# Delta-rule attention and SwiGLU on one core: the first group's diagonal blocks as 64x32 products of their own, one transpose, and other engines for beta's products and two clearings

## The chip, the cores and the metric

The kernel runs on one core of one Trainium2 chip. The metric is the device time of one execution in microseconds. A kernel is judged by the median of its runs; the profile is one more execution, recorded by the hardware profiler.

Engine names in the views: PE is TensorE (PEld its weight loads), DVE is VectorE, ACT is ScalarE, POOL is GpSimd, SP is SyncE, which here only issues DMAs. L444 is line 444 of the kernel file.

## The reference, cut to what matters

```python
# q, k, v: (4, 8, 768, 48), beta: (4, 8, 768), float32
def attn(q, k, v, beta):
    k_n = k / (np.linalg.norm(k, axis=-1, keepdims=True) + 1e-06)
    state = zeros((B, H, D, D))
    for t in range(S):
        kt, vt, bt = k_n[:, :, t], v[:, :, t], beta[:, :, t, None]
        y[:, :, t] = einsum('bhd,bhde->bhe', q[:, :, t], state)
        v_old = einsum('bhde,bhd->bhe', state, kt)
        state = state + bt[..., None] * einsum('bhd,bhe->bhde', kt, vt - v_old)
    return y
# bridge: (B, H, S, D) -> x of (3072, 384); then
def moe(x, w_gate, w_val, w_out):           # 384 -> 1536 -> 384
    g = x @ w_gate
    return (g / (1 + exp(-g))) * (x @ w_val) @ w_out
```

## The kernel before, in words

The sequence of 768 steps is cut into 12 chunks of C = 64 steps; two chunks make a group. Four batches with eight heads are 32 recurrences. Within a chunk the recurrence is solved with the triangular matrix of the keys' products: the Gram matrix K K' of each recurrence's chunk (64 x 64) is scaled by beta and inverted as a unit triangular matrix. The inverse is made in 32 x 32 blocks (R = 32): the two diagonal blocks of a chunk by forward substitution on VectorE, all recurrences of a group at a time, one per partition, and the block below the diagonal by two rounds of small products on TensorE (`join_late`, L561 to L592).

**The start, which the change touches.** It is written out by hand under a manual schedule (from L1094), so each engine executes its instructions in the order of the code. Group 0 goes first:

- The keys of chunks 0 and 1 are loaded, and beta in 16 small DMAs, eight on POOL's queue and eight on SP's (`load_beta`, L377). VectorE forms the keys' squared norms (`norms`, L353, L361), GpSimd takes their square root as a power of 0.5 (L365).
- TensorE turns the keys (L432), ScalarE copies them to SBUF (L434), and `gram` (L444) makes the 64 x 64 Gram matrices of both chunks: 32 matmuls a chunk with 64 x 64 stationary tiles, of which four are in use (two halves of the rows, two halves of the columns). A float32 matmul leaves two records in the trace.
- L472 copies them from PSUM into `a_sb`, for group 0 in the layout (i, chunk, head), one strided copy for each bank: three on VectorE and one on ScalarE.
- `turn` (L479) brings the diagonal blocks into the form in which one partition holds one recurrence: a transpose over 128 partitions (L482) for one half, and two over 32 partitions each (L485) for the other.
- `first_n` (L386 to L390) makes the reciprocal norms from GpSimd's result, L1128 copies beta out of the place it was loaded to, `divide_beta` (L369) multiplies beta twice by the reciprocal norm, and `scale_m` clears `zb` and puts beta on its diagonal (GpSimd, L497, L498), negates beta (L500) and scales `mb` with it (L502).
- `substitute` (L510) is 31 steps of two VectorE instructions each (L515, L521), every one waiting for the one before it. After 17 of the steps, four small instructions (L246) that prepare the weights' conversion are put between.
- `late_z` (L552, L558) transposes the result into `zt` and `d_t`; `join_late` starts on TensorE with L568, then L580; ScalarE copies the blocks (L588); then come `advance(0)` (L716, L735, L747) with the first chunk's outputs, their transposes (L780, L783), and the first gate products (L800).

While that goes on, TensorE turns q and the next keys (L432), makes their products (L444), and turns group 1's diagonal blocks by 32 x 32 products with the identity (`turned_m`, L544). The weights arrive as 64-bit floats, as pairs of words; `convert` (L246 to L296) makes float32 of them with VectorE and ScalarE.

**The rest.** From the first gate product on, TensorE works through the feed-forward products of every chunk: gate and value (L800), output (L829, L912). Between them, `fill` and `point` put steps of the recurrence of later chunks and of the next groups' inverses, in an order fixed at build time.

PSUM has eight banks: the pairs `px` and `py`, and four banks `ffn`. The Gram products of chunks 0 and 1 use `px` and `py`, and the turned keys of chunks 2 and 3 come next in the same two pairs.

The start as it stands in the code, from L1115:

```python
        copy_a, copy_v = nc.scalar.copy, nc.vector.tensor_copy
        turned(0, False)
        turned(1, False, "py")
        gram(0, False)
        gram(1, False, "py", (copy_a, copy_v))
        mb = new_mb()
        ...
        r_b = first_n()
        copy_v(beta_b, beta_s.rearrange("p (g r) -> p g r", g=NG)[:, :, 0:R])
        ...
        divide_beta(0, r_b)
        zb = scale_m(mb, [(slice(0, R), mb)], beta_b[:, 0])
        nc.gpsimd.memset(ztp[0], 0.0)
```

Of the kernel before, what the change touches and what calls it, by code (L numbers as in the profile page):

```python
# [21 lines left out]
def kernel(  # L22
# [350 lines left out]
    def load_beta(at, queue=nc.gpsimd):  # L373

        s_, blk, c, par = at // 8, at // 4 % 2, at // 2 % 2, at % 2
        lo, m = 64 * c + R * blk, (NG - 1) * 128 + R
        queue.dma_start(  # L377
            out=beta_s[8 * at : 8 * at + 8, 0:m],
            in_=beta.rearrange("(bp b) (j par) s -> b par bp j s", b=2, par=2)[
                s_ ^ par, par, :, :, lo : lo + m  # L380
            ],
        )

    def first_n():
        n = n_t[0].rearrange("p c h -> p (c h)")
        nc.vector.tensor_scalar_add(n, n, 1e-6)  # L386
        r_n = work.tile([128, R], FP32, name="r_n", tag="n_b", bufs=1)
        nc.vector.reciprocal(r_n, n)
        r_b = work.tile([128, R], FP32, name="r_b", tag="nb", bufs=1)
        nc.vector.transpose(r_b, r_n)  # L390
        return r_b
# [46 lines left out]
    def gram_steps(c, of_q, tag=None, copies=(nc.vector.tensor_copy,) * 2):  # L438

        xt = (qt if of_q else kt)[c]  # L440
        p_g = banks("p_g", tag or ("py" if of_q else "px"))
        p_v = [p.rearrange("p (bp j i) -> p bp j i", bp=NB, j=NJ) for p in p_g]
        for bp, j, par, b, _ in every():
            nc.tensor.matmul(  # L444
                p_v[par][half_of(b if of_q else b ^ par), bp, j],
                kt[c][half_of(par), bp, j, b],
                xt[half_of(par), bp, j, b],
            )
        if of_q:
            p_sb[c] = work.tile([128, 2, NB, NJ, C], FP32, name="p_sb", bufs=2)  # L450
        elif c % 2 == 0:
            a = work.tile([128, C * 2 * HH], FP32, name="a_sb")

            a_sb[c // 2] = (
                a.rearrange("p (i c h) -> p c h i", c=2, h=HH)
                if c == 0
                else a.rearrange("p (c h i) -> p c h i", c=2, h=HH)
            )
            a_of[c // 2] = a
        yield  # L460
        for par in range(2):
            p_h = p_g[par].rearrange("p (h i) -> p h i", i=C)
            if of_q:
                nc.vector.tensor_tensor(
                    out=p_sb[c][:, par].rearrange("p bp j i -> p (bp j) i"),
                    in0=p_h,
                    in1=mask_q[:, None, :].to_broadcast([128, HH // 2, C]),
                    op=ALU.mult,
                )
            else:  # L470
                at = slice(par * HH // 2, (par + 1) * HH // 2)
                copies[par](a_sb[c // 2][:, c % 2, at], p_h)  # L472
        yield

    def gram(*args):
        for _ in gram_steps(*args):
            pass

    def turn(out, in_):  # L479


        nc.vector.transpose(out(slice(0, 128), 1), in_(slice(0, 128), 1))  # L482
        yield
        for rows in (slice(0, 32), slice(64, 96)):
            nc.vector.transpose(out(rows, 0), in_(rows, 0))  # L485
            yield
# [23 lines left out]
    def substitute(mb, zb):  # L510
        for j in range(R - 1):
            m = R - 1 - j
            tmp = work.tile([128, 256], FP32, name="tmp", bufs=1)
            t_v = tmp[:, 0 : (j + 1) * m].rearrange("p (k i) -> p k i", i=m)
            nc.vector.tensor_tensor(  # L515
                out=t_v,
                in0=zb[:, 0 : j + 1, j : j + 1].to_broadcast([128, j + 1, m]),
                in1=mb[:, j : j + 1, j + 1 : R].to_broadcast([128, j + 1, m]),
                op=ALU.mult,
            )  # L520
            nc.vector.tensor_tensor(  # L521
                out=zb[:, 0 : j + 1, j + 1 : R],
                in0=zb[:, 0 : j + 1, j + 1 : R],
                in1=t_v,
                op=ALU.add,
            )
            yield

    def recur(p, m=D):
        p = p[:, :, 0 : NB * NJ * m]  # L530
# [556 lines left out]
    with tc.manual_schedule(  # L1087
# [9 lines left out]
        for at in range(0, 16, 2):  # L1097
            load_beta(at)
            load_beta(at + 1, nc.sync)
        norms(0)  # L1100

        nc.vector.memset(places[0][:, 0:1], 0)
# [12 lines left out]
        copy_a, copy_v = nc.scalar.copy, nc.vector.tensor_copy  # L1115
        turned(0, False)
        turned(1, False, "py")
        gram(0, False)
        gram(1, False, "py", (copy_a, copy_v))
        mb = new_mb()  # L1120
        a_v = a_of[0].rearrange("p (i m) -> p i m", i=C)
        for _ in turn(
            lambda rows, half: mb[rows],
            lambda rows, half: a_v[rows, R * half : R * half + R],
        ):
            pass
        r_b = first_n()
        copy_v(beta_b, beta_s.rearrange("p (g r) -> p g r", g=NG)[:, :, 0:R])  # L1128
        for n in range(12, 17):
            stage(n)  # L1130
        load_v(1)
        divide_beta(0, r_b)
        zb = scale_m(mb, [(slice(0, R), mb)], beta_b[:, 0])
        nc.gpsimd.memset(ztp[0], 0.0)

        turned(0, True, "ffn")
        turned(2, False, "px")
# [111 lines left out]
```

## Time and profile before

| what | value |
|---|---|
| median of 8 runs | 749.32 us (747.34 to 750.08) |
| profiled execution | 749.11 us |
| its span, first to last instruction | 747.4 us |
| busy in the span | PE 709.0, PEld 616.3, DVE 475.4, ACT 149.4, POOL 68.0 us |
| mean granted clock of TensorE | 0.961 |
| first substitution step (L515) starts | 22.92 us after the span's start |
| last substitution step (L521) ends | 46.92 us |
| first product of the join (L568) starts | 49.09 us |
| first gate product (L800) starts | 66.87 us |

The profile page gives busy time by engine, the span in 40 slices, the chain of work that ended last, and groups of instructions with what their engine waited for. Queries of the same trace give the chain in order of time, all instructions of a window in order of time (start, duration, engine, line, operation, then in brackets the idle time before it and what ended that), the waits summed by pair, and busy time and granted clock by window. Times there count from the span's start. The profiled execution's own time is 1.7 us above its span. The granted clock of a window is a share of TensorE's full clock.

### The profile page before, as it was taken

The page shows a single profiled execution, that of the slowest core. Times are in us where ns is not written, and L with a number is a line of the kernel's source. Part 1 is how long each engine was busy: PE and PEld are TensorE (multiplying, and loading weights), DVE is VectorE, ACT ScalarE, POOL GpSimd, SP SyncE. Part 2 cuts the span into 40 slices and gives each one's busy share as a digit, 9 for nine tenths or more (in the row PEclk, how much of TensorE's full clock was granted, in tenths as well). Part 3 has the DMA queues.
Part 4 walks back from the last instruction along what each step waited for, and adds up shares of the span by engine and source line. Part 5 has one row for each costly group of instructions (what it writes and reads, how often), then busy time and mean ns, then how long its engine had stood idle before and what let it go on. Part 6 is the DMA issues. An engine that isn't in the chain of part 4 may idle for free.

```text
span 747.4 us, 22217 instructions
## 1 busy us (share of the span) xinstructions
PE 709.0 (95%) x10004; PEld 616.3 (82%) x10004; DVE 475.4 (64%) x981; ACT 149.4 (20%) x277; POOL 68.0 (9%) x46
## 2 busy tenths in 40 slices
PE   4747999999999999999999999999999999999997
PEld 3636888866788688988988988988988988989987
DVE  6899888979378453478863478864478754313122
ACT  2346434211311111112011112011112011021010
POOL 7107200200300000030000030000030000000000
PEclk9555999999999999999999999999999999999999
DMA  7774533130203002331301331401220200000000
GB/s 154 178 219 118 140 78 121 59 53 23 55 13 54 13 19 32 48 58 32 54 14 20 47 62 27 60 7 25 42 47 1 42 3 3 22 3 0 22 1 21
DMA packets 130734, 37.17 MB, mean 50 GB/s; under 512 B 122864, under 2 KB 125936, under 8 KB 130640
## 3 DMA queue, kind: packets, MB, share of 16 engines
q1 hardware_dynamic: 127184, 34.01, 22.1%
q10 hardware_dynamic: 3072, 1.57, 1.0%
q8 instruction: 78, 1.28, 0.7%
q0 software_dynamic: 384, 0.17, 0.1%
q14 instruction: 16, 0.13, 0.1%
HBM read 31.01 MB, written 4.72 MB: 48 GB/s over the span
## 4 chain that ended last, share of the span: by engine, by line
PE 82%; DVE 12%; issue 2%; SPq 1%; DMA 1%; ACT 1%; ACTq 0%; DVEq 0%
PE p_gate L800 24%; PE p_val L800 23%; PE p_o L912 14%; PE p_o L829 6%; DVE tmp L515 3%; DVE zb L521 3%; PE p_g L444 2%; PE p_j L580 2%; PE p_y L735 2%; PE p_u L716 2%; PE p_s L747 2%; PE p_r L695 1%; PE p_y L704 1%; DVE h_f L870 1%; DVE h_f L815 1%
## 5 line engine op out<-in xcount | busy, mean ns | idle before, releaser
L800 PE MATMUL p_gate<-x_ffn,wg_sb 128*128 128x256 f32 x864 | 208.0, 392 | 1.4 <-ACT x_ffn L783 1.4
L800 PE MATMUL p_val<-x_ffn,wv_sb 128*128 128x256 f32 x864 | 198.5, 379 | 0.0
L800 PEld LDWEIGHTS p_gate<-x_ffn,wg_sb 128*128 128x128 f32 x864 | 163.7, 194 | 25.2 <-ACT x_ffn L783 2.0
L800 PEld LDWEIGHTS p_val<-x_ffn,wv_sb 128*128 128x128 f32 x864 | 163.8, 190 | 22.3
L815 DVE TENSOR_TENSOR h_f<-sil,p_val 128x512 f32<-128x512 f32 x71 | 48.5, 684 | 152.0 <-PE p_val L800 151.5
L809 ACT ACTIVATE sil<-p_gate 128x512 f32<-128x512 f32 x72 | 43.0, 598 | 281.5 <-PE p_gate L800 257.9
L608 POOL TENSOR_TENSOR n_b<-mb,half 128x32 f32<-128x32 f32 x5 | 42.2, 8437 | 411.0 <-DVE mb L485 373.2
L912 PE MATMUL p_o<-wo_sb,h_f 128*128 128x192 f32 x432 | 75.6, 328 | 0.1
L515 DVE TENSOR_TENSOR tmp<-zb,mb 128x31 f32<-128x31 f32 (+15 forms) x186 | 63.3, 340 | 16.0 <-PE p_j L580 10.8
L912 PEld LDWEIGHTS p_o<-wo_sb,h_f 128*128 128x128 f32 x432 | 70.3, 190 | 1.2 <-DVE o_sb L922 0.7
L521 DVE TENSOR_TENSOR zb<-zb,tmp 128x31 f32<-128x31 f32 (+15 forms) x186 | 63.7, 343 | 6.4
L922 DVE TENSOR_TENSOR o_sb<-o_sb,p_o 128x192 f32<-128x192 f32 x45 | 15.8, 350 | 53.7 <-PE p_o L912 36.5
L829 PE MATMUL p_o<-wo_sb,h_f 128*128 128x384 f32 x136 | 45.7, 490 | 0.0
L829 PEld LDWEIGHTS p_o<-wo_sb,h_f 128*128 128x128 f32 x136 | 25.3, 190 | 16.5
L912 PE MATMUL p_o<-last_k,h_f 128*128 128x192 f32 x180 | 32.2, 326 | 0.0
L912 PEld LDWEIGHTS p_o<-last_k,h_f 128*128 128x128 f32 x180 | 29.7, 190 | 0.0
L870 DVE TENSOR_TENSOR h_f<-h_f,h_f 128x256 f32<-128x256 f32 x54 | 22.4, 424 | 8.0 <-PE p_o L912 7.1
L912 PE MATMUL p_o<-last_h,h_f 128*128 128x192 f32 x144 | 26.3, 326 | 0.0
L912 PEld LDWEIGHTS p_o<-last_h,h_f 128*128 128x128 f32 x144 | 23.9, 190 | 0.0
L254 ACT ACTIVATE last_h<-last_h,rebias 128x512 int32<-128x512 uint32 (+2 forms) x26 | 15.3, 616 | 31.6 <-DVE last_h L246 31.6
L485 DVE STREAM_TRANSPOSE mb<-a_sb 32x1024 f32<-32x1024 f32 x10 | 19.5, 1950 | 0.3
L716 PEld LDWEIGHTS p_u<-vin,zt 64*64 64x64 f32 x768 | 13.4, 141 | 6.1 <-issue 3.2
(163 smaller groups left out, 683.3 us busy)
## 6 DMA issues: line engine op xcount, KB each, us to landing
vin<-in_v_dram SPq DMA_DIRECT2D x96, 48.0 KB
kn<-in_k_dram SPq DMA_DIRECT2D x40, 96.0 KB
out_dram<-o_sb SPq DMA_DIRECT2D x36, 96.0 KB
zt<-in_moe_w_out_dram SPq DMA_DIRECT2D x6, 384.0 KB
staged<-in_moe_w_out_dram SPq DMA_DIRECT2D x6, 384.0 KB
qpad<-in_q_dram SPq DMA_DIRECT2D x36, 64.0 KB
wo_sb<-in_moe_w_gate_dram SPq DMA_DIRECT2D x4, 512.0 KB
wo_sb<-in_moe_w_val_dram SPq DMA_DIRECT2D x4, 512.0 KB
```

What stands on the lines that cost most here:

```text
L485: nc.vector.transpose(out(rows, 0), in_(rows, 0))
L515: nc.vector.tensor_tensor(out=t_v, in0=zb[:, 0 : j + 1, j : j + 1].to_broadcast([128, j + 1, m]), in1=mb[:, j : j + 1, j + 1 : R].to_broad ...
L521: nc.vector.tensor_tensor(out=zb[:, 0 : j + 1, j + 1 : R], in0=zb[:, 0 : j + 1, j + 1 : R], in1=t_v, op=ALU.add,)
L608: nc.gpsimd.tensor_tensor(out=n, in0=mb.rearrange("p j i -> p (j i)")[:, 0 : R * R : R + 1], in1=half, op=ALU.pow,)
L716: nc.tensor.matmul(p_u[half_of(b), par, bp, j], zt[half_of(b ^ par), par, bp, j], r[half_of(b ^ par), par, bp, j], start=first, stop=True, ...
L800: nc.tensor.matmul(ps[name][:, i], w_sb[:, t, (f + i) * 128 : (f + i + 1) * 128], xts[c][:, t], start=(t == 0), stop=(t == KT - 1),)
L809: nc.scalar.activation(sil, ps[name], ACTF.Silu)
L815: nc.vector.tensor_tensor(out=hs[c, f], in0=sil, in1=ps["p_val"], op=ALU.mult)
L829: nc.tensor.matmul(p_o, hs[c, f - f % 2][:, f % 2, bp * 128 : (bp + 1) * 128], wo_sb[:, f], start=(f == 0), stop=(f == FT - 1),)
L870: nc.vector.tensor_tensor(out=out, in0=a, in1=b, op=ALU.subtract)
L912: nc.tensor.matmul(p[x, part], a(f - f % 2)[:, f % 2], b(f), start=not begun and f == 0, stop=f == FH - 1, skip_group_check=True,)
L922: nc.vector.tensor_tensor(out=out, in0=a, in1=b, op=ALU.add)
```

## The change

Five things are done to group 0 alone; later groups keep their code.

1. Group 0's Gram products are replaced by `first_gram`. Each 64 x 64 block of a recurrence is made by two matmuls: the upper diagonal 32 x 32 block (32 stationary columns, 32 moving), and the two lower blocks (32 stationary columns, 64 moving). So there are 64 matmuls a chunk in place of 32, and the stationary tile is 64 x 32. The outputs are laid out so that both diagonal blocks stand in one part of the PSUM bank, in all four quarters of the partitions.
2. `first_diag` copies only the diagonal blocks into the first 1024 columns of `a_sb`: four copies of 256 columns, two on ScalarE and two on VectorE. One transpose over 128 partitions replaces the three. `first_below` copies the blocks below the diagonal afterwards: four ScalarE copies over 32 partitions of 512 columns.
3. The copy of beta moves from VectorE to ScalarE, between the first and the second of ScalarE's diagonal copies; `first_n` moves ahead of the last diagonal copy on VectorE.
4. The two products of beta with the reciprocal norm move from VectorE to GpSimd, ahead of beta's copy to the diagonal of `zb`.
5. The clearings of `zb` (128 x 1024) and `ztp[0]` (128 x 2048) move from GpSimd to VectorE, to its start, ahead of the norms.

```diff
@@ gram_steps: the layout that only group 0 had is gone
-            a_sb[c // 2] = (
-                a.rearrange("p (i c h) -> p c h i", c=2, h=HH)
-                if c == 0
-                else a.rearrange("p (c h i) -> p c h i", c=2, h=HH)
-            )
+            a_sb[c // 2] = a.rearrange("p (c h i) -> p c h i", c=2, h=HH)
@@ new functions
+    def first_tiles():
+        a = work.tile([128, C * 2 * HH], FP32, name="a_sb")
+        first_of["flat"] = a[:, 0 : R * R]
+        first_of["diag"] = a[:, 0 : R * R].rearrange("p (j h) -> p h j", j=R)
+        a_sb[0] = a[:, R * R :].rearrange("p (c h j) -> p c h j", c=2, h=HH)
+        zb = work.tile([128, R, R], FP32, name="zb", bufs=1)
+        nc.vector.memset(zb, 0.0)
+        nc.vector.memset(ztp[0], 0.0)
+        first_of["zb"] = zb
+
+    def first_gram(c, tag):
+        p_g = ps_pair("p_g", tag)
+        p_v = p_g.rearrange("p par (x h i) -> p par x h i", x=2, i=R)
+        for bp, j, par, b, _ in every():
+            k_v = kt[c][half_of(par), bp, j, b].rearrange("p (x i) -> p x i", x=2)
+            h, s_ = NJ * bp + j, b ^ par
+            hi, lo = slice(64 * s_, 64 * s_ + R), slice(64 * s_ + R, 64 * s_ + C)
+            nc.tensor.matmul(p_v[hi, par, 1, h], k_v[:, 0], k_v[:, 0])
+            nc.tensor.matmul(p_v[lo, par, :, h], k_v[:, 1], k_v)
+        return p_g, p_v
+
+    def first_diag(c, par, p, copy):
+        at = HH * c + HH // 2 * par
+        copy(first_of["diag"][:, at : at + HH // 2], p[1][:, par, 1])
+
+    def first_below(c, p):
+        for lo in (slice(R, C), slice(64 + R, 64 + C)):
+            nc.scalar.copy(
+                a_sb[0][lo, c].rearrange("p (par h) j -> p par (h j)", par=2),
+                p[0][lo, :, 0 : HH // 2 * R],
+            )
+
+    def first_scale(mb, r_b):
+        zb, b = first_of["zb"], beta_b[:, 0]
+        nb = work.tile([128, R], FP32, name="nb", tag="nb_1", bufs=1)
+        for _ in range(2):
+            nc.gpsimd.tensor_tensor(out=b, in0=b, in1=r_b, op=ALU.mult)
+        nc.gpsimd.tensor_copy(zb.rearrange("p k i -> p (k i)")[:, 0 : R * R : R + 1], b)
+        nc.vector.tensor_scalar_mul(nb, b, -1.0)
+        nc.vector.tensor_tensor(
+            out=mb, in0=mb, in1=nb[:, None, :].to_broadcast([128, R, R]), op=ALU.mult
+        )
+        return zb
@@ the start
+        first_tiles()
         norms(0)
...
-        gram(0, False)
-        gram(1, False, "py", (copy_a, copy_v))
+        p_g = [first_gram(0, "px"), first_gram(1, "py")]
+        first_diag(0, 0, p_g[0], copy_a)
+        first_diag(0, 1, p_g[0], copy_v)
+        copy_a(beta_b, beta_s.rearrange("p (g r) -> p g r", g=NG)[:, :, 0:R])
+        first_diag(1, 0, p_g[1], copy_a)
+        r_b = first_n()
+        first_diag(1, 1, p_g[1], copy_v)
         mb = new_mb()
-        a_v = a_of[0].rearrange("p (i m) -> p i m", i=C)
-        for _ in turn(
-            lambda rows, half: mb[rows],
-            lambda rows, half: a_v[rows, R * half : R * half + R],
-        ):
-            pass
-        r_b = first_n()
-        copy_v(beta_b, beta_s.rearrange("p (g r) -> p g r", g=NG)[:, :, 0:R])
+        nc.vector.transpose(
+            mb.rearrange("p j i -> p (j i)"), first_of["flat"]
+        )
...
-        divide_beta(0, r_b)
-        zb = scale_m(mb, [(slice(0, R), mb)], beta_b[:, 0])
-        nc.gpsimd.memset(ztp[0], 0.0)
+        zb = first_scale(mb, r_b)
+        for c in range(2):
+            first_below(c, p_g[c])
```

## The prediction, made before the changed kernel was run

> **What bounds the kernel now.** I read the waits of TensorE from 60 us on first (who waited for whom: total, times, longest):
>
> ```profile
> PE p_f L780 <- ACT y L770: 2.1, 1, 2.1
> PE p_gate L800 <- ACT x_ffn L783: 1.4, 2, 0.9
> PE p_u L716 <- DVE vin L712: 0.7, 1, 0.7
> PE p_y L735 <- ACT uu L727: 0.7, 1, 0.7
> ```
>
> That is all up to 300 us, and the page has PE at 9 tenths to the end. So from the first gate product (66.87 us) the kernel is TensorE's work in a fixed order, and a start that comes earlier ends earlier by as much. What sets the start is in the chain in order of time (start, duration, engine, line):
>
> ```profile
> 20.63 0.27 DVE beta_b L1128
> ...
> 21.59 1.24 DVE mb L502
> ...
> 22.92 0.20 DVE tmp L515
> ...
> 46.71 0.22 DVE zb L521
> ...
> 47.03 1.92 DVE zt L552
> ...
> 49.09 1.86 PE p_j L568 x58
> ```
>
> The 24 us of substitution are VectorE's alone and the change leaves them. What counts is when they start: 22.92. VectorE ahead of that, from the timeline:
>
> ```profile
> 11.67 1.89 DVE L472 COPY a_sb<-p_g 128x512 f32<-128x512 f32 x2 [0.37 <-PE p_g L444]
> 14.42 1.01 DVE L472 COPY a_sb<-p_g 128x512 f32<-128x512 f32 x1 [0.86 <-ACT a_sb L472]
> 15.47 1.25 DVE L482 STREAM_TRANSPOSE mb<-a_sb 128x1024 f32<-128x1024 f32 x1
> 16.75 2.48 DVE L485 STREAM_TRANSPOSE mb<-a_sb 32x1024 f32<-32x1024 f32 x2
> 19.26 0.18 DVE L386 TENSOR_SCALAR n_t<-n_t 128x32 f32<-128x32 f32 x1
> ```
>
> From 14.42 on it runs without a pause, except 0.55 us ahead of L1128. The view blames a DMA for that, but eight semaphore instructions stand on VectorE's queue from 19.9 to 20.5: beta came by 16 DMAs, and checking 16 semaphores takes that long. Beta itself had landed (last issue on GpSimd's queue at 7.3, landing 4.6 us later at most). And GpSimd:
>
> ```profile
> 8.76 6.50 POOL L365 TENSOR_TENSOR n_t<-n_t,half 128x16 f32<-128x16 f32 x2 [0.86 <-DVE h_f L1102]
> ...
> 21.50 0.24 POOL L498 COPY zb<-beta_b 128x32 f32<-128x32 f32 x1 [5.34 <-DVE beta_b L369]
> ```
>
> The roots are ready at 15.26, four microseconds before VectorE asks for them. In the changed kernel they are what it waits for.
>
> **The change, part by part.**
>
> *VectorE's path.* Its order is now: one diagonal copy, `first_n`, the second diagonal copy, one transpose, beta's negation, the scaling, substitution.
> - `first_n` starts when the roots are there, about 15.30, and takes 0.82 (19.26 to 20.08 before): 16.12.
> - The copy queued behind this wait has half the columns with the same stride of 32 elements as L472's 1.02 us: 0.51, to 16.67 with a 0.04 gap. Nobody else waits for VectorE meanwhile but GpSimd's products.
> - The transpose is L482's: 1.25, to 17.96. The two of L485 (16.75 to 19.26: 2.51) are gone.
> - From the start of L500 to the first L515 it was 21.38 to 22.92, 1.54 us, and stays so: the substitution starts at 19.52.
>
> So it comes 22.92 - 19.52 = **3.4 us** earlier. As a check: 2.51 for the transposes, 1.30 for semaphores, beta's copy and two products (20.08 to 21.38), 0.82 for `first_n`, now ahead of the transpose, less 1.24 by which that one starts later (16.71 against 15.47): 3.39.
>
> *TensorE's products.* This has a cover. ScalarE's copy of chunk 1's first diagonal half must end by 16.12, so the second product must end by about 15.55. The rows:
>
> ```profile
> 9.62 3.69 PE L444 MATMUL p_g<-kt 64*64 64x64 f32 x128
> ...
> 30.57 0.71 PE L444 MATMUL p_g<-last_k 64*64 64x64 f32 x16 [2.20 <-issue]
> 32.47 3.89 PE L544 MATMUL p_m<-ident,a_sb 32*32 32x32 f32 x240 [1.19 <-ACT a_sb L472]
> 38.85 0.45 PE L544 MATMUL p_m<-ident,a_sb 32*32 32x32 f32 x16 [2.49 <-issue]
> ```
>
> Now there are 256 records. They were 28.8 ns each with 64x64 tiles (3.69/128), are 16.2 with four 32x32 tiles in turn (3.89/240), and 31 with two (L568, 64 in 2.00 at 72.97). The new order goes through eight tiles. I take 16 ns, the row with the smallest tiles in turn and the most of them: 4.1 us, the second product done at 13.8. The cover holds up to (15.55 - 9.62 - 0.1)/256 = 22.8 ns. At 28.8 the end is 17.1 and 1.5 us of the gain go; at 31, 17.7 and 2.1 us. Below 16 nothing is gained, since the roots are then the later.
>
> A rule speaks against these tiles. In the Trainium skill, "TensorE: Matmul & The Clock Gate", Part 3, "The mechanism", a weight load overlaps running matmuls only when it goes to other rows of the array, and the two tiles of a pair here stand on the same rows; by its figures for a load (32/1.2 ns) and a cold matmul (N/1.2 ns, 40 ns on average) that would be an estimated 4.3 us for each product and leave a gain of some 0.7 us. But the 64x64 products of this trace already have two tiles on each half of the rows and take 1.85 us a product, where the same rule gives an estimated 3.4; I go by the row.
>
> *TensorE's instructions.* The two idle times "<-issue" above, and 1.17 us at 52.05, come without a wait on any engine. They stand before the 344th, 600th and about the 728th matmul record, multiples of 128 plus 88, and the page's instruction queue moved 78 packets of 16 KB: stretches of code that came late. The 216th record is such a place too. Before, TensorE idled there from 13.3 to 17.5 anyway; now it falls into the second product. A full gap of 2.2 to 2.5 us ends that product at 16.0 to 16.3 and costs 0.5 to 0.8 us. DMA was light when it would be asked for (share 0.13 from 9.5 to 10.5), so I take no cost, and keep this as a case. The 128 added records are just one such stretch, so the later places stay where they are.
>
> *Beta on ScalarE.* After its first diagonal copy (about 11.9 to 12.4): 0.6 for the semaphores, 0.32 for 128x192 (L768's row), done at 13.4. Queued behind it is the diagonal copy of chunk 1, which has no product before 13.8. It costs nothing unless beta lands after about 15.
>
> *Beta's products on GpSimd.* From 16.2, two products and the copy to `zb`. The trace has no such product. Below stands the copy of the same shape, 0.24; above, the power, 6.2. VectorE asks for the result at 17.98, so each may take 0.89 free of charge, and the gain is gone at 2.6. I take 0.24, the row with as little arithmetic. VectorE's work slows GpSimd (the power took 17.35 at 61.24 beside the conversions, 6.21 elsewhere), but 2.8 times 0.24 is still under 0.89.
>
> *Clearings on VectorE.* They lie in its idle 4.93 us before 5.93. 3072 columns at the tensor-tensor row's rate (1.23 for 1024) are 3.7, at the conversion's (0.42 for 512) 2.5: they end by 4.7 at the latest. If they held up GpSimd's own start, it would be by at most 3.7, which shifts beta's issue and the roots; the roots would be later by at most 2.8 (11.6 in place of 8.76), and so would the substitution. No row shows a clearing that does so; I take zero.
>
> *The blocks below.* Four ScalarE copies at 0.58 (L588's row) end about 17.9: the last two follow VectorE's copy at 16.67. They free the PSUM pairs for the next keys, which TensorE turns from 19.37 on, when these have landed. Nothing there is late.
>
> *What is late next.* `zt` is ready at 45.5 rather than 48.94. TensorE's earlier work ends at 41.2 (39.23 + 1.97), ScalarE's at 42.4 (41.38 + 1.04); v is scaled at 41.5. The conversions follow VectorE's order; its waits from 45 to 300 us name no DMA, and the first piece that they read late in the loads (58.25, now 54.85) had landed: DMA share is 0.04 from 54 to 60. So the whole shift reaches the gate products.
>
> **The sum.** 749.11 - 3.4 = 745.7 for the profiled execution, which is 0.2 under the median of the runs; against the median, 749.32 - 3.4 = **745.9 us**. About 0.2%, 1.5 us, is what a measurement of this kernel can tell from no change. The granted clock moves this: it is 0.5 until 71.7 and again 0.53 from 82.0 to 85.3, where gate products (L800) took 4.54 us in place of 2.86. Another position of the work against such a stretch gains or loses up to 1.7.
>
> **Rivals.**
> - *Code comes late in the second product* (16%). For: three such gaps in the first 54 us. Against: light DMA there. Gain 2.6 to 2.9 by this alone; the later gap at 52 us may grow by as much as 1.2 when moved into busier DMA (share 1.0 up to 46.5): 746.4 to 747.9, still over 0.2% as a rule.
> - *The tiles run at the pair's 31 ns, or the roots are held up* (13%). For: no row shows eight tiles. Gain 0.6 to 1.4: 747.9 to 748.7, within 0.2%.
> - *The narrow tiles run only two at a time, at their own length* (9%, slower). A tile with 64 moving columns takes 4 x 28.8 = 115 ns in the 64x64 row, with 32 columns 4 x 16.2 = 65; two at a time that is 45 ns a record, 11.5 us in all, the second product done at 21.3, 5.7 us after the cover ends: 2.3 slower, 751.6. It decides from 36 ns on (3.4 us past the cover). Against: four tiles do run side by side in both rows.
> - *The forecast* (62%): gain 2.9 to 5.1, the upper end with one slow stretch of the clock fewer: 744.2 to 746.4.
>
> The range, 744.2 to 748.3, leaves out the slower case and part of the third. Faster 0.78 (forecast and late code), same 0.13, slower 0.09.
>
> **What would show it.** Right: the first L510 (L515 before) at 19.3 to 19.8; VectorE idle until 15.3 and then released by GpSimd's root; the products of GpSimd done before the transpose is; the join at about 45.7 and the first gate product at about 63.5. Wrong: VectorE's second diagonal copy released by ScalarE, and behind it by TensorE (tiles or code); beta's negation released by GpSimd; a join that starts early but gate products that don't.

## The result, and the profile after

The median after is **745.09 us** (13 runs, 743.06 to 746.29) beside 748.38 us for the kernel before (36 runs): ratio 0.9956, 95% interval 0.9945 to 0.9967, so 3.3 us less (2.5 to 4.1). The profiled execution took 743.06 us, its span 741.4.

Line numbers are now those of the changed kernel: first substitution step L510 (L515 before), join L612 and L624 (L568, L580), first gate product L844 (L800), the new products L546 and L547, the diagonal copies L552, the one transpose L1171.

TensorE's waits from 60 to 300 us (engine, line, releaser: total, times, longest) are those of before with other line numbers (the wait of p_y now lies ahead of 60 us), so a start that comes earlier still ends earlier:

```profile
PE p_f L824 <- ACT y L814: 2.1, 1, 2.1
PE p_gate L844 <- ACT x_ffn L827: 1.8, 2, 0.9
PE p_u L760 <- DVE vin L756: 0.7, 1, 0.7
```

VectorE from 12 us on, in order of time (start, duration; the brackets hold the idle time ahead and what ended it):

```profile
12.59 0.59 DVE L552 COPY a_sb<-p_g 128x256 f32<-128x256 f32 x1 [0.97 <-ACT a_sb L552]
15.61 0.18 DVE L386 TENSOR_SCALAR n_t<-n_t 128x32 f32<-128x32 f32 x1 [2.43 <-POOL n_t L365]
...
17.00 0.59 DVE L552 COPY a_sb<-p_g 128x256 f32<-128x256 f32 x1 [0.58 <-ACT a_sb L552]
17.63 1.25 DVE L1171 STREAM_TRANSPOSE mb<-a_sb 128x1024 f32<-128x1024 f32 x1
18.79 0.14 DVE L567 TENSOR_SCALAR nb<-beta_b 128x32 f32<-128x32 f32 x1
18.97 1.23 DVE L568 TENSOR_TENSOR mb<-mb,nb 128x1024 f32<-128x1024 f32 x1
20.30 0.19 DVE L510 TENSOR_TENSOR tmp<-zb,mb 128x31 f32<-128x31 f32 x1
```

The substitution starts at 20.30, 2.62 us earlier, and not at 19.52. The reason is the third line shown: the second diagonal copy is released by ScalarE, 0.58 us after `first_n` is done. The chain that ended last, in order of time, tells what ScalarE waited for:

```profile
12.67 2.61 issue
15.72 0.64 PE p_g L547 x14
16.39 0.59 ACT a_sb L552
17.00 0.60 DVE a_sb L552
17.63 1.25 DVE mb L1171
```

TensorE stood for 2.61 us inside the second product, after 220 matmul records of the program, with no wait that the profile shows ("issue"). Records are numbered from 0 here, so the one that came late is record 220. A packet of 16 KB on the instruction queue went out at 12.81.

The join and TensorE's products behind it:

```profile
46.41 1.76 PE L612 MATMUL p_j<-zt,a_sb 32*32 32x32 f32 x58 [4.11 <-DVE zt L596]
...
63.30 4.28 PE L844 MATMUL p_gate<-x_ffn,wg_sb 128*128 128x256 f32 x12 [0.95 <-ACT x_ffn L827]
67.51 1.15 PE L791 MATMUL p_s<-uu,kn 64*64 64x48 f32 x64
68.59 1.20 PE L612 MATMUL p_j<-zt,a_sb 32*32 32x32 f32 x64
```

The last row took 2.00 us before, in the same place and at the same granted clock (1.00):

```profile
72.97 2.00 PE L568 MATMUL p_j<-zt,a_sb 32*32 32x32 f32 x64
```

Nothing in the prediction speaks of it.

Where the profiled execution gained, read from the starts of the same work in both traces: first substitution step 2.62; join 2.68; first L760 product 3.57 (a gap ahead of the join's second half is 0.50 us in place of 1.17); first gate product 3.57; the products behind the second join 5.19 (0.8 from the row above, the rest from where the half clock ended); end of the span 6.0 (before had one more stretch at half clock, 3.4 us long, from 208.0). The gap inside the join and the clock stretches differ between executions of the same code. The other two parts, 2.6 and 0.8, make 3.4, and the median fell by 3.3. The 2.6 is read from one execution of each kernel; in two kernels below with the same code up to there (e1 and e8) the first step came at 20.16 and 20.07.

### The profile page after: what moved, and what is told of

It reads as the page before. It is cut to its first block, busy times and chain, and to the rows that moved or that the text cites. A ratio compares the mean times of both kernels' runs of the same rounds, so it can differ in the third digit from the quotient of the medians.

```text
span 741.4 us, 22478 instructions
## 1 busy us (share of the span) xinstructions
PE 705.9 (95%) x10132; PEld 613.9 (83%) x10132; DVE 473.1 (64%) x977; ACT 152.6 (21%) x283; POOL 67.2 (9%) x46
## 4 chain that ended last, share of the span: by engine, by line
PE 81%; DVE 16%; issue 2%; DMA 1%; ACT 0%; SPq 0%; ACTq 0%; DVEq 0%
PE p_gate L844 23%; PE p_val L844 22%; PE p_o L956 15%; PE p_o L873 6%; DVE tmp L510 3%; DVE zb L516 3%; PE p_g L444 2%; PE p_u L760 2%; PE p_r L739 1%; PE p_s L791 1%; PE p_y L779 1%; PE p_y L748 1%; PE p_j L624 1%; DVE h_f L914 1%; DVE last_h L287 1%
## 5 line engine op out<-in xcount | busy, mean ns | idle before, releaser
L844 PE MATMUL p_gate<-x_ffn,wg_sb 128*128 128x256 f32 x864 | 205.9, 389 | 1.8 <-ACT x_ffn L827 1.8
L844 PE MATMUL p_val<-x_ffn,wv_sb 128*128 128x256 f32 x864 | 198.5, 379 | 0.0
L844 PEld LDWEIGHTS p_gate<-x_ffn,wg_sb 128*128 128x128 f32 x864 | 162.2, 192 | 24.9 <-ACT x_ffn L827 2.3
L844 PEld LDWEIGHTS p_val<-x_ffn,wv_sb 128*128 128x128 f32 x864 | 163.8, 190 | 22.3
L510 DVE TENSOR_TENSOR tmp<-zb,mb 128x31 f32<-128x31 f32 (+15 forms) x186 | 63.3, 340 | 16.3 <-PE p_j L624 11.1
L760 PEld LDWEIGHTS p_u<-vin,zt 64*64 64x64 f32 x768 | 13.4, 141 | 6.0 <-issue 3.2
L480 DVE STREAM_TRANSPOSE mb<-a_sb 32x1024 f32<-32x1024 f32 x8 | 17.1, 2135 | 0.2
```

What stands on the lines that cost most here:

```text
L510: nc.vector.tensor_tensor(out=t_v, in0=zb[:, 0 : j + 1, j : j + 1].to_broadcast([128, j + 1, m]), in1=mb[:, j : j + 1, j + 1 : R].to_broad ...
L760: nc.tensor.matmul(p_u[half_of(b), par, bp, j], zt[half_of(b ^ par), par, bp, j], r[half_of(b ^ par), par, bp, j], start=first, stop=True, ...
L844: nc.tensor.matmul(ps[name][:, i], w_sb[:, t, (f + i) * 128 : (f + i + 1) * 128], xts[c][:, t], start=(t == 0), stop=(t == KT - 1),)
```

## The experiments

Two questions were open. **Why 20.30 and not 19.52:** my theory was code that comes late (a stretch of instructions that is not there yet when TensorE reaches it), the rival a limit of the narrow tiles or of the copies. **Why the second join is 0.8 us shorter:** my theory was the new layout of the blocks below the diagonal, whose 32 elements of one weight load lie side by side now.

Landmarks from the traces (us from the span's start). "Product" is the start of the last record of the second Gram product.

| kernel | roots ready | product | first step | join | first L760 | first gate | median | ratio to before, interval |
|---|---|---|---|---|---|---|---|---|
| before | 15.26 | 13.00 | 22.92 | 49.09 | 56.77 | 66.87 | 748.38 | 1 |
| after | 15.57 | 16.04 | 20.30 | 46.41 | 53.20 | 63.30 | 745.09 | 0.9956, 0.9945 to 0.9967 |
| e1_strided_below | 15.74 | 16.00 | 20.16 | 46.28 | 53.36 | 63.46 | 746.1 | 0.9957, 0.9939 to 0.9974 |
| e2_early_120 | 17.35 | 16.10 | 21.37 | 47.51 | 54.66 | 64.76 | 746.67 | 0.9978, 0.9964 to 0.9991 |
| e2_early_184 | 17.87 | 15.62 | 21.89 | 48.01 | 54.08 | 64.19 | 745.84 | 0.9952, 0.9933 to 0.9971 |
| e5_rest_without_tiles | 14.98 | 13.74 | 22.05 | 48.16 | 54.95 | 65.06 | 746.72 | 0.9966, 0.9952 to 0.998 |
| e3_beta_vector | 15.31 | 16.01 | 20.72 | 46.83 | 53.62 | 63.73 | 744.18 (one run) | |
| e4_clear_gpsimd | 14.68 | 15.97 | 20.38 | 47.10 | 53.75 | 63.86 | 747.76 (one run) | |
| e6_loads_after_first_copy | 15.62 | 14.78 | 19.64 | 46.93 | 55.66 | 65.75 | 747.1 | 0.9983, 0.9968 to 0.9997 |
| e8_contiguous_dt | 15.38 | 15.90 | 20.07 | 46.16 | 53.06 | 63.17 | 740.36 | 0.9899, 0.9882 to 0.9915 |
| e10_dt_and_later_loads | 14.49 | 14.89 | 19.06 | 45.15 | 53.15 | 63.25 | 741.0 | 0.9915, 0.9898 to 0.9932 |
| e11_keys_before_weights | 15.23 | 14.67 | 19.27 | 45.37 | 54.74 | 64.85 | 742.04 | 0.9922, 0.9906 to 0.9939 |

Each median stands beside runs of before on the same chip; chips differ, so kernels are compared by ratios.

### The blocks below the diagonal, strided again

```diff
-        a_sb[0] = a[:, R * R :].rearrange("p (c h j) -> p c h j", c=2, h=HH)
+        a_sb[0] = a[:, R * R :].rearrange("p (j c h) -> p c h j", c=2, h=HH)
...
-                a_sb[0][lo, c].rearrange("p (par h) j -> p par (h j)", par=2),
-                p[0][lo, :, 0 : HH // 2 * R],
+                a_sb[0][lo, c].rearrange("p (par h) j -> p par h j", par=2),
+                p[1][lo, :, 0],
```

> The changed kernel with the blocks below the diagonal stored in the old order again (neighbours of one block 32 elements apart), all else as changed. Theory A (part of the gain is that the join reads these blocks as weights, and that a strided weight load is slower): the second join's first products take 2.0 us again in place of 1.20, the substitution still starts at 20.3 +- 0.3 us, ScalarE's four copies of the blocks take about 4 us in place of 2.36 without anybody waiting, and the time is some 0.8 us above the changed kernel. Theory B (the 1.20 comes from the granted clock at that place): it stays at 1.20 and the time is the changed kernel's.

The second join, at the full clock, in order of time of this kernel's TensorE:

```profile
69.80 2.00 PE L612 MATMUL p_j<-zt,a_sb 32*32 32x32 f32 x64
```

2.00 us again, as before, with everything else of the change in place: the layout makes the difference. The weight loads' own records say the same: on average 144 ns a load here and 145 before, 108 in the changed kernel. At half clock the first join shows little of it (first to last record 1.79 against 1.68; at the full clock, in the second, 1.79 against 1.01). ScalarE's four copies took 4.21 us and nobody waited. The time cannot confirm 0.8 us: the interval of this kernel is 2.6 us wide and holds the changed kernel's ratio.

### Products put at the program's start, to move the places where code runs out

```diff
+        p_early = ps_ffn([128, 512], "p_early")
+        for n in range(60):
+            quad = QUADS[n % 4][0]
+            nc.tensor.matmul(p_early[quad, 0:R], half[quad], half[quad])
         turned(0, False)
```

The products work on a constant and nobody uses their result; 60 of them are 120 records, 92 (in the second kernel) are 184.

> The changed kernel with 60 idle 32x32 products (120 records) of a constant ahead of TensorE's first transpose, in time in which it waits for the keys; their result is not used. Theory A (the 2.61 us of idle time inside the second narrow product is code that comes late): the idle time sits at a fixed number of records from the start of the program, so the stretch that ended at record 220 now ends at the 84th record of the two products and was asked for before they began, and the next gap can only come at about the 212th; some of the 2.61 us go, and the substitution starts between 19.5 and 20.3 us. Theory B (the gap belongs to the product, by PSUM, the copies of the turned keys or the narrow tiles): it stays after 204 records of the products and keeps its 2.6 us, with the substitution at 20.3.

> As the run with 60 idle products, with 92 of them (184 records). Theory A: the ends of the stretches fall on about the 20th and the 148th record of the two products; no gap at the 204th; if one comes at the 148th, it starts by 12.3 us and the second product ends by about 15.5, so that the substitution starts at 19.5 to 19.9 us, and the time is 0.4 to 0.8 us under the changed kernel. Theory B: a gap of 2.6 us after 204 records, and no change.

The gap did what the theory says of its place. It stood ahead of record 220 of the program in the changed kernel and of record 348 in both of these, one stretch of 128 further, although 212 records of the products lie ahead of it in the one kernel and 148 in the other. A limit of the tiles would have stayed at a place of the product, and did not. It was 2.15 and 1.15 us from record to record, against 2.83.

Nothing was gained, though: the substitution started at 21.37 and 21.89, and both theories had it at 20.3 or earlier. The stretch that had been fetched at 12.8 was now fetched at 4.69 and 4.88 us, while the keys were being loaded, and VectorE got the keys 1.8 and 2.3 us later than at 6.24; in the second kernel:

```profile
8.54 0.96 DVE L353 TENSOR_TENSOR ksq<-kn 128x768 f32<-128x768 f32 x1 [4.32 <-DMA kn<-in_k_dram]
...
17.91 0.18 DVE L386 TENSOR_SCALAR n_t<-n_t 128x32 f32<-128x32 f32 x1 [3.34 <-POOL n_t L365]
```

The roots came later by as much and became the bound. The packet itself took only 1.3 us; how it holds the keys for 1.8 to 2.3 is not shown. In the second kernel the gap inside the join was gone as well (join to first L760: 6.07 us, in place of 6.80). Its first gate product came 0.89 later than the changed kernel's; the median doesn't show that, and its interval is too wide to.

### Everything but the tiles and the single transpose

Group 0 gets the products, the copies, the three transposes and the strided layout of before back; beta's copy on ScalarE, its products on GpSimd, the clearings on VectorE stay.

```diff
-        p_g = [first_gram(0, "px"), first_gram(1, "py")]
+        gram(0, False)
+        gram(1, False, "py", (copy_a, copy_v))
...
-        nc.vector.transpose(mb.rearrange("p j i -> p (j i)"), first_of["flat"])
+        for _ in turn(
+            lambda rows, half: mb[rows],
+            lambda rows, half: a_v[rows, R * half : R * half + R],
+        ):
+            pass
```

> The kernel before with the other parts alone: the copy of beta on ScalarE, the reciprocal norms ahead of the transposes, beta's products on GpSimd, both clearings on VectorE; the Gram products stay 64x64 and the three transposes stay. Theory A (the start adds up on VectorE as predicted): the path loses 1.30 us of semaphores, copy and products, so that the substitution starts at about 21.6 us; the second join's first products keep their 2.0 us; time about 1.3 us under the kernel before, so that the tiles with the single transpose and the order of the blocks below are worth the other 2 us. Theory B (what gains is the lighter GpSimd or the earlier clearing, not VectorE's path): the time is that of the changed kernel.

First step at 22.05, 0.87 earlier than before, and 0.45 later than I had expected. VectorE's path hangs from the start of the products here, and they started 0.74 later in this execution (10.36 against 9.62): with that taken out, moving beta is worth 1.6 us. What the tiles and the one transpose add is 1.75 by the two first steps, held down by the late code. The intervals overlap: by the medians this kernel is 2.5 us (1.5 to 3.6) under the kernel before and the changed one 3.3 (2.5 to 4.1). So the split rests on the traces alone, one execution of each.

### Beta's products on VectorE, and the clearings on GpSimd

```diff
-            nc.gpsimd.tensor_tensor(out=b, in0=b, in1=r_b, op=ALU.mult)
+            nc.vector.tensor_tensor(out=b, in0=b, in1=r_b, op=ALU.mult)
```

> beta's two products go back to VectorE (0.2 us each), the copy to zb stays on GpSimd. My theory: on GpSimd they lay in the shadow of the second diagonal copy and the transpose, so that on VectorE they are two more instructions on the path, which lie between the transpose and the negation: the first substitution product at 20.7 to 20.9 (20.30 in the changed kernel), the scaling 0.4 to 0.6 later. Rival: GpSimd's products (0.29 each) and its copy were what the negation waited for: the substitution starts within 0.1 of 20.30 or earlier.

This kernel's VectorE, in order of time:

```profile
18.77 0.38 DVE L565 TENSOR_TENSOR beta_b<-beta_b,r_b 128x32 f32<-128x32 f32 x2
19.18 0.18 DVE L567 TENSOR_SCALAR nb<-beta_b 128x32 f32<-128x32 f32 x1
```

The first step came at 20.72: with the products' end at 16.01 (16.04 in the changed kernel) that is 0.45 later, the two products with their gap. On GpSimd they took 0.58 for both in the changed kernel, from 16.57, and nothing waited for them.

The clearings, in another kernel: `zb`'s ahead of beta's products, `ztp[0]`'s behind the copy to `zb`'s diagonal.

```diff
-        nc.vector.memset(zb, 0.0)
-        nc.vector.memset(ztp[0], 0.0)
...
+        nc.gpsimd.memset(zb, 0.0)
...
+        nc.gpsimd.memset(ztp[0], 0.0)
```

> The clearings of zb and of group 0's zt go back to GpSimd, the first ahead of beta's products, the second behind the copy to zb, as they stood before the change. My theory: VectorE's clearings lie in time in which it waits for the keys anyway, and zb's clearing on GpSimd (0.94) fits while the roots are awaited or shortly after, so the move is worth at most 0.3 us here: substitution starts at 20.2 to 20.6, and the norms of the keys end within 0.3 us of where they did. Rival: the clearing on GpSimd stands between the power and the products, and the negation waits for it: the substitution starts at 21.0 or later.

Substitution at 20.38: the move of the clearings is worth nothing measurable as things stand. GpSimd and VectorE of this kernel show that the two do meet:

```profile
14.63 0.94 POOL L561 MEMSET zb<- 128x1024 f32 x1
16.39 0.58 POOL L564 TENSOR_TENSOR beta_b<-beta_b,r_b 128x32 f32<-128x32 f32 x2 [0.82 <-DVE r_b L390]
```

```profile
14.71 0.90 DVE L386 TENSOR_SCALAR n_t<-n_t 128x32 f32<-128x32 f32 x1 [1.48 <-POOL n_t L365]
```

A VectorE instruction of 0.18 us took 0.90 and ended when GpSimd's clearing did. It cost nothing because TensorE was still the later.

### Loads held until the first diagonal copy

SyncE's first load waits for a one-column clearing on VectorE; here this clearing, and with it the loads of the code, stand behind the first diagonal copy.

```diff
-        nc.vector.memset(places[0][:, 0:1], 0)
         norms(1)
-        for n in range(4):
-            stage(n)
-        load_q(0)
-        ...
         first_diag(0, 1, p_g[0], copy_v)
+        nc.vector.memset(places[0][:, 0:1], 0)
+        for n in range(4):
+            stage(n)
+        load_q(0)
+        ...
```

> SyncE's loads (the first four weight pieces, q, the keys of chunks 2 and 3, and what follows) are held until VectorE has copied its first diagonal block, by moving the one-column clearing that they wait for behind that copy; nothing else moves. The DMA is then idle from about 9.7 to 12.5 us, when the stretch of code is fetched that TensorE lacks at its 220th record. My theory (the stretch is asked for about when the 92nd record goes by, at 11.0, and comes late because the DMA rings are full: 1.85 us to the packet, another 2.47 to the first record): the packet at 11.6 to 12.0, the gap 1.0 to 1.8 us in place of 2.83, the second product done at 14.4 to 15.1, the substitution started by the roots at 19.5 to 19.7, 0.6 to 0.8 earlier. The loads come 3 us later, before the first products that use them wait. Time 744.0 to 745.2. Rival: the fetch takes its 4 us whatever else is loaded: gap 2.6 to 2.9, substitution at 20.2 to 20.4, time 744.8 or more, later where late loads are waited for.

Busy time by window: start and end, length, then busy us with instruction counts for PE, PEld, DVE, ACT, POOL, the granted clock, the DMA share and GB/s. First the changed kernel, then this one:

```profile
11.00:12.00 1.00, 1.00 (x102) 1.00 (x93) 0.60 (x2) 0.20 (x2) 1.00 (x1) 1.00 0.84 274
12.00:13.00 1.00, 0.67 (x65) 0.51 (x51) 0.41 (x1) 0.90 (x2) 1.00 (x2) 1.00 1.07 389
13.00:14.00 1.00, 0.00 (x0) 0.00 (x0) 0.18 (x1) 0.00 (x0) 1.00 (x1) 1.00 0.91 271
14.00:15.00 1.00, 0.00 (x0) 0.00 (x0) 0.00 (x0) 0.00 (x0) 1.00 (x1) 1.00 1.02 238
```

```profile
11.00:12.00 1.00, 1.00 (x107) 1.00 (x96) 0.65 (x2) 0.26 (x2) 1.00 (x1) 1.00 0.15 43
12.00:13.00 1.00, 0.73 (x69) 0.57 (x52) 0.42 (x1) 0.90 (x2) 1.00 (x2) 1.00 0.00 0
13.00:14.00 1.00, 0.00 (x0) 0.00 (x0) 0.17 (x2) 0.00 (x0) 1.00 (x1) 1.00 0.00 0
14.00:15.00 1.00, 0.75 (x52) 0.58 (x51) 0.00 (x0) 0.00 (x0) 1.00 (x1) 1.00 0.50 143
```

The reader is to see the last column but one: with the DMA full from 11 on (share 0.84 to 1.07) TensorE stood still until 15.28; with the DMA empty it stood still too, but until 14.25. The packet went out 0.75 us after the 92nd record (128 before the 220th) instead of 1.85, and 2.48 against 2.47 us passed from packet to the first record. So a fetch has a part that the DMA's load sets and a part of 2.5 us that it doesn't, and 128 records at 13 ns (1.7 us) are through before that. The roots were there at the same time (15.62 against 15.57), and this kernel's VectorE went on from them without a wait:

```profile
15.65 0.18 DVE L386 TENSOR_SCALAR n_t<-n_t 128x32 f32<-128x32 f32 x1 [2.48 <-POOL n_t L365]
...
16.39 0.55 DVE L552 COPY a_sb<-p_g 128x256 f32<-128x256 f32 x1
...
19.64 0.19 DVE L510 TENSOR_TENSOR tmp<-zb,mb 128x31 f32<-128x31 f32 x1
```

The substitution started at 19.64: **the late code cost 0.66 us**. That 19.64 lies within 0.12 of the forecast of 19.52 is two small misses that nearly cancel: the roots' use began 0.35 later than forecast, and the path from there was 0.23 shorter.

The time got worse, because the loads came 3.5 us later. TensorE turned q at 21.14 in place of 18.12, ScalarE's last copies of q ended 3.4 us later, and the join waited for these copies and started at 46.93, 0.5 later than in the changed kernel:

```profile
46.94 1.76 PE L612 MATMUL p_j<-zt,a_sb 32*32 32x32 f32 x58 [1.22 <-ACT qt L434]
```

Then the gap inside the join was 2.41 in place of 0.50.

### The inverse laid out side by side

```diff
-        z_late[g] = work.tile([128, R, 2 * HH], FP32, name="d_t", tag="p_sb", bufs=2)
-        nc.vector.transpose(z_late[g], zb)
+        z_late[g] = work.tile([128, 2 * HH, R], FP32, name="d_t", tag="p_sb", bufs=2)
+        nc.vector.transpose(z_late[g].rearrange("p m k -> p k m"), zb)
...
-                        d_t[hi, :, HH * c + h],
+                        d_t[hi, HH * c + h],
```

> The copy of the inverse that join_late loads as TensorE's weights is laid out so that the 32 elements of one load lie side by side, as the change did for the blocks below the diagonal; the transpose that makes it then writes in steps of 32 elements (1.9 in place of 1.2 us on VectorE, two times). My theory: what went from 2.00 to 1.20 us in the second join is the stride of the weights in memory; the same form with strided weights runs there at 28 ns a record at the full clock, and is to fall to 19: 0.6 us for each 64 records, twice in group 0's second join and four times in group 1's, 3.6 us in all. Time 741.0 to 742.5. Rival: the gain of the second join came from something else in the blocks below (their place in the tile, the copies that end earlier), or VectorE's 0.7 more is waited for: 28 ns stay, time 744.7 to 746.0.

Group 1's join on TensorE, first in the changed kernel, then in this one:

```profile
200.08 2.00 PE L624 MATMUL p_j<-ident,d_t 32*32 32x32 f32 x64
201.92 1.98 PE L624 MATMUL p_j<-t,d_t 32*32 32x32 f32 x64
203.83 2.43 PE L844 MATMUL p_gate<-x_ffn,wg_sb 128*128 128x256 f32 x10
```

```profile
198.68 1.20 PE L624 MATMUL p_j<-ident,d_t 32*32 32x32 f32 x64
199.71 1.18 PE L624 MATMUL p_j<-t,d_t 32*32 32x32 f32 x64
200.82 2.86 PE L844 MATMUL p_gate<-x_ffn,wg_sb 128*128 128x256 f32 x12
```

From the first join product to the gate product behind it: 3.75 us, now 2.14, so 0.8 for each 64 records and not the 0.6 that I had expected. Six such sets run at the full clock: 4.8 us. The ratio is 0.9899, 0.57% (4.3 us) below the changed kernel's, the lowest of all, and the two intervals don't touch. VectorE's longer transpose (1.2 to 1.9 us) cost nothing that can be seen: from the join to the first L760 product, less the gap in between, it is 6.26 us here and 6.29 in the changed kernel. This settles the second question, on another operand and at another place: at the full clock, TensorE's weights are loaded more slowly when their elements lie 128 bytes apart. At the full clock the records of these weight loads take 145 ns on average with the strided copy and 108 with the contiguous one, and a product's record starts every 28 ns and every 16.

### The same with later loads

```diff
-        nc.vector.memset(places[0][:, 0:1], 0)
         norms(1)
+        nc.vector.memset(places[0][:, 0:1], 0)
```

> The contiguous copy of the inverse as before, and SyncE's loads held only until VectorE has done the second chunk's norms (about 11.6 us in place of 13.2 in the run that held them behind the first diagonal copy; 9.7 without a hold). The code of the 220th record is asked for at about 11.0 and went out at 11.8 when the DMA was idle. My theory: that packet still goes out ahead of the loads (11.7 to 12.0), the gap is 1.6 to 2.0, the substitution starts at 19.5 to 19.8, and the loads, 1.9 us later than without a hold, bring q and the keys early enough that the join still waits for VectorE (45.6 to 46.0): 0.3 to 0.6 us below the contiguous copy alone, 739.7 to 740.1. Rival: with loads 1.9 us later TensorE's products of chunks 2 and 3 and ScalarE's copies of q still end after VectorE's transpose, as with the longer hold, so the join starts at 46.1 or later: 740.3 to 742.

In the second kernel three of the first four weight pieces are loaded behind q and the keys:

```diff
-        for n in range(4):
-            stage(n)
+        stage(0)
         load_q(0)
         load_k(2)
         load_k(3)
-        for n in range(4, 10):
+        for n in range(1, 10):
             stage(n)
```

> As the run beside it, but of the four weight pieces that are held only the first stays ahead of q and of the keys of chunks 2 and 3; the other three are loaded behind them. TensorE gets q and the keys 1.3 us earlier than in the run beside it, the pieces come some 10 us later, ahead of the conversions at 33 us. My theory: if the join of the run beside it was late for q or the keys, it is released by VectorE here, at 45.6 to 46.0, and the time is 739.7 to 740.1; if not, both are equal within 0.5 us. Rival: the pieces then come too late for the powers in the middle of the substitution, and conversions fall behind after the join: first gate product at 63.5 or later, 740.5 to 742.

The start came out as I said: packets at 11.61 and 11.37 (0.75 and 0.74 after the 92nd record), first steps at 19.06 (roots at 14.49) and 19.27, and a join that waits for VectorE. The whole is no faster all the same. TensorE of the first of the two:

```profile
45.15 1.92 PE L612 MATMUL p_j<-zt,a_sb 32*32 32x32 f32 x64 [2.70 <-DVE zt L596]
46.86 1.22 PE L624 MATMUL p_j<-ident,d_t 32*32 32x32 f32 x37
49.83 0.90 PE L624 MATMUL p_j<-ident,d_t 32*32 32x32 f32 x26 [1.75 <-issue]
...
53.15 0.45 PE L760 MATMUL p_u<-vin,zt 64*64 64x48 f32 x4 [0.66 <-ACT zt L632]
```

The join starts 1.0 us earlier than with the contiguous copy alone (45.15 against 46.16), and the first L760 product 0.1 later (53.15 against 53.06): the gap at the next boundary of code took all of it. The packet for that stretch went out 0.99 us after the join's start in the changed kernel and 1.30 in the one with the contiguous copy, where the DMA share from 46 to 48 us was 0.64 and 0.74; it was 1.83, 3.34 and 2.54 in these two and in the one with the longer hold, with shares of 1.08, 1.03 and 1.03. The two go together in these five executions; no run changes the load at this place alone. So my theory of these two runs held for the start and fell for the time, and neither rival named the reason: in the first the products of chunks 2 and 3 were in time, and in the second the code, not the conversions, made the first gate product late (64.85). The ratios (0.9915 and 0.9922) are not told from 0.9899 by their intervals.

## Why the prediction was right, and where it was not

The forecast was 745.9, the time 745.09, a gain of 3.3 us for 3.4. The sign and the mechanism were right; the agreement of the sums is partly luck: the shift of the start was 2.6 and not 3.4, and a term of 0.8 was missing.

- *TensorE sets the end, and a shift of the substitution reaches it:* right. 2.62 us at the first step were 2.68 at the join and 3.57 at the first gate product.
- *VectorE's path:* right. It was idle until the roots came (released by GpSimd at 15.61). With the late code made shorter, the path from `first_n` to the first step took 3.99 us (15.65 to 19.64) for 4.22. The small sizes that were off: the half copy took 0.55 to 0.59 for 0.51; it began 0.74 after the start of `first_n`, with 0.86 in the sum, and the negation 1.17 after the start of the transpose, with 1.27 in the sum; the roots came 0.3 later (keys at 6.24 for 5.93; the kernels with the same code up to there gave 5.82 to 6.38).
- *Narrow tiles at 16 ns a record:* right, and on the safe side. 204 records ran from 9.95 to 12.67, 13.3 ns each, at a granted clock of 1.00. The rows that the prediction compares were not alike: the one at 16.2 ns ran at a granted clock of 0.50, those at 28.8 and 31 at 1.00. The last 52 records of the changed kernel's products ran at 0.50 and started every 14.9 ns; in the kernel with the loads held they ran at 1.00 and started every 10.4. Both are well under the 22.8 ns up to which the cover holds. The rule of the Trainium skill that spoke against them ("TensorE: Matmul & The Clock Gate", Part 3, "The mechanism": a load overlaps running matmuls only on other rows) does not describe these tiles: it gave an estimated 4.3 us a product, and 128 records at 13.3 ns are 1.7. That estimate took the page's figure for a cold matmul, although the granted clock was 1.00; with its figure for a warm one (N/2.4 + 2.5 ns) it would be an estimated 3.1 us, still nearly twice the measured time.
- *"so I take no cost" for the code at the 216th record:* **this step failed.** The gap came at record 220, 2.61 us of idle time (2.83 from record to record), and cost 0.66. I had read the DMA share of 0.13 from 9.5 to 10.5 us, but the packet went out only after the 92nd record, which passed at 11.0, and by then SyncE's loads had filled the DMA; and an empty DMA would still have left 1.73 from record to record, since the part of the fetch that is not load is 2.5 us and faster tiles use up a stretch in 1.7. The prediction's remark that TensorE idled at this place before anyway is not what the trace shows: in the kernel before, record 216 passed at 25.73, 12.6 us after the packet (13.14), so no gap could show there. The 128 added records brought the place into the product, and the tiles' speed left the code no time. This was the case that I gave 16%; its price for this gap, 0.5 to 0.8, was right, and so was the sign named for it, a second diagonal copy released by ScalarE with TensorE behind it. That the time lies in the forecast's range (744.2 to 746.4) and not in this case's (746.4 to 747.9) is luck: the missing term below made up for it. On the chip's page on running code ("Runtime: NRT & Kernel Launch", "Instruction fetch mechanics") the Trainium skill says that instructions come in blocks of 256 ahead of use, and that this is mostly hidden; the size agrees with gaps every 128 loads and 128 matmuls, the hiding does not hold here.
- *The missing term:* the new layout of the blocks below the diagonal takes the second join from 2.00 to 1.20 us. The prediction costed the copies that make the layout and not the loads that read it. The row was there to be read in the trace before: group 1's join, which had the contiguous layout already, took 1.20 for the same 64 records.
- *Beta on ScalarE, its products on GpSimd:* right (0.35 and 0.58 us, nobody waits). The 0.6 that the sum has for the semaphores was not paid: ScalarE's eight semaphore instructions ran from 11.95 to 12.51, beside its diagonal copy of 11.94 to 12.55, and beta's copy began at 12.54. With the products back on VectorE the step comes 0.45 later.
- *Clearings free:* right, 0.91 and 1.76 us (2.7 in all, at the lower of the two bounds) in VectorE's idle time, done at 4.21.
- *"The later places stay where they are":* right (records 471, 599, 727 and 853 for 344, 472, 600 and 726). Their length went with where the DMA's load fell: the one in the join could have grown by 1.2 and shrank by 0.67 in this execution; it was 1.75, 2.41 and 3.13 in the three kernels with later loads.
- *Rivals:* the tiles at the pair's 31 ns, or at two at a time, are refuted by 13.3 ns; the roots were not the later until the code was made faster.

## What to carry to other kernels

When a change makes TensorE's instructions faster, ask whether their code arrives as fast: here 128 matmul records passed in 1.7 us and the next stretch of code was there 3.0 to 4.6 us after the boundary before, the later the more bulk loads were issued at that moment. Cost a new layout at its readers too, weight loads above all: of this change's layouts the one that was a by-product was worth 0.8 us, and the same step taken for the operand beside it 4.3 us. And what is won ahead of the next late stretch of code may be given back there, so read the second gap before the first is removed.

## What the runs showed of the hardware

- Late code: gaps on TensorE at fixed records of the program, 128 apart, of 0.5 to 3.0 us in the changed kernel and up to 4.96 in the one with the clearings on GpSimd; some of the places pass without one. For the first such gap, from the record 128 ahead of it to the packet 0.74 to 0.75 us with a nearly idle DMA and 1.4 to 1.9 with loads; from the packet to the first record 2.3 to 2.9 us in either case.
- A code packet that fell into the loading of the keys (4.7 to 4.9 us) went with keys that landed 1.8 to 2.3 us later.
- 64x32 tiles on the same rows ran beside each other: 13.3 ns a record at the full clock (28.8 with the 64x64 tiles of before at the full clock, 16.2 with four 32x32 tiles at half clock).
- Two 32x32 tiles in turn with weights whose elements lie 128 bytes apart: 1.77 to 1.79 us from the first of 64 records to the last at the full clock; side by side: 0.99 to 1.01. At half clock, in the first join, 1.79 and 1.68: the clock made no difference with the strided weights and a large one with the others. A weight load's record took 145 and 108 ns at the full clock.
- Eight semaphore instructions took 0.56 us on ScalarE; they ran beside the copy ahead of them and cost nothing.
- A VectorE instruction of 0.18 us took 0.90 beside a GpSimd clearing of 0.94 and ended with it.
